# B's attention in pieces of four PSUM banks instead of two

## The chip, the core and the metric

The kernel runs on one core of a Trainium2 chip. The time is the device time of one execution in microseconds (us). A core has five engines that run their own instruction streams and wait for each other through semaphores: TensorE (PE in the profile, its weight loads PEld), VectorE (DVE), ScalarE (ACT), GpSimd (POOL) and SyncE (SP, which here only issues DMA transfers). TensorE writes its results to PSUM, eight banks of 512 fp32 numbers for each of 128 partitions; ACT and DVE read them from there.

## What is computed

Two attention blocks over the same `x` (2048 rows of 1024 numbers), mixed row by row with a gate. Block A is linear attention, block B looks at eight earlier positions at distances 0, 2, ... 14. Both have 32 heads of 32 numbers.

```
g = sigmoid((x * gate_w).sum(-1))
A:  phi(t) = where(t > 0, t + 1, exp(t)) + 1e-6
    kv = einsum("bhsd,bhse->bhde", phi(k), v);  z = phi(k).sum over s
    a  = (phi(q) @ kv) / (phi(q) . z + 1e-6) @ A_wo
B:  idx = pos - (0, 2, ... 14);  logits = q . k[idx] * 32**-0.5, masked where idx < 0
    b  = (softmax(logits) @ v[idx]) @ B_wo
out = g * a + (1 - g) * b
```

## The kernel before

**Products.** Rows are split into even and odd positions (`p` is 0 or 1), so that B's dilated window is eight neighbours within one half. The large matrix products (q, k, v of A and B and the output projections) run in groups with seven block products instead of eight (`Group`: `m1` to `m7`). In the projections, each of the seven is four matmuls of 128x128x512 into a PSUM tile called X or Y; there are two X and two Y tiles of one bank each (pool `ps_pj`). ACT copies X out (`save`, M1s, U2s, U4s), DVE adds Y to such a copy, and the next product of that tile has to wait for it. `run` (line 403) issues a group's products with the last two of the group before it woven in.

**Side work.** Between products, `side` lets small pieces of other work in: B's attention (`attn`), the sums K'V of A (`kv` in `va_group`) and A's outputs (`out` in `qa_out`). Each is a Python generator that issues one piece and then yields two numbers: the delay, in products, before its next piece, and the hold, the number of products for which that piece will keep its PSUM tile. `step` (line 334) takes the first piece that is due and whose tile is free by that count. The counts are only a plan: on the chip, a piece waits by semaphore until the engines have read its PSUM tile. The remaining four banks are two tiles of two banks, `ps_s` and `ps_o`, and a piece takes the one that has been free longest (lines 328 to 332).

**B's attention.** An item is one of eight pairs (chunk pair `nn`, half `p`); it covers eight heads, four in each of two chunks. It handles three stretches `t` of 342 positions. Each is cut into six blocks of 57 (3 `j` x 2 `b`), and a block looks at 64 keys. `scores(t, r)` (line 656) makes the scores of two heads for both chunks: 24 matmuls with 32 rows and 64 columns of the array each, on four array tiles (two heads times two `b`). ACT takes Exp of 684 numbers a partition (line 672), DVE multiplies with the mask (line 674). `pv(t, ch, pts)` (line 677) makes the results of four heads of one chunk: 24 matmuls with V and eight with ones for the denominators, on eight array tiles. ACT takes Ln of the denominators and Exp of minus that (lines 696, 697), DVE multiplies (line 698), SP stores (line 699). Four tiles `PT` are used in turn. So each stretch takes two score pieces and two pv pieces; an item has twelve pieces.

**A's sums and outputs.** `kv` (line 529) adds the sums of 8 column blocks in two pieces, of 12 and 4 matmuls, each followed by a DVE add into `KVacc`. `out` (line 570) does two pieces of four matmuls, each copied by ACT (line 585).

**Order.** The order on TensorE and SP is that of the program text. On ACT, DVE and POOL a scheduler chooses the order at build time; each engine then executes in that order. With every DVE add of the products, `issue_after` keeps deferred sums (`xsums`, `Weights.sums`) behind it. phi (line 501) runs an Exp over 1024 numbers on ACT (line 503) and three operations on DVE for every row tile of A's keys.

The gate's sums `gps` live in a tile of `ps_o` (line 425), and the 20 warm-up matmuls in one of `ps_s` (line 830).

Of the kernel before, what the change touches and what calls it, by code (L numbers as in the profile page):

```python
# [9 lines left out]
ALU = mybir.AluOpType  # L10
# [4 lines left out]
P = 128  # L15
# [13 lines left out]
def kernel(  # L29
# [41 lines left out]
    ps_o = ctx.enter_context(tc.tile_pool(name="ps_o", bufs=1, space=bass.MemoryType.PSUM))  # L71
# [6 lines left out]
    ptp = ctx.enter_context(tc.tile_pool(name="ptp", bufs=1))  # L78
# [147 lines left out]
    PTs = []  # L226
    for i in range(4):
        PTs.append(ptp.tile([P, 2, TW], BF16, name=f"PT{i}"))

# [87 lines left out]
    state = {"credit": 0.0, "prev": None, "steps": 0, "now": 0}  # L317
# [10 lines left out]
    free = {"s": 0, "o": 0}  # L328

    def ps_tile(name):  # L330
        tag = state["tag"]
        return (ps_s if tag == "s" else ps_o).tile([P, 2, 512], F32, name=name, tag=tag)

    def step(force=False):
        seen = set()
        for entry in list(queue):
            if entry[4] in seen:
                continue
            seen.add(entry[4])
            tag = min(free, key=free.get)  # L340
            if not force and (entry[0] > state["now"] or free[tag] > state["now"]):
                continue
            free[tag] = state["now"] + entry[3]
            state["tag"] = tag
            try:
                delay, entry[3] = next(entry[1])
                entry[0] = state["now"] + delay
                state["steps"] += 1
                return True
            except StopIteration:  # L350
                queue.remove(entry)
                return step(force)
        return False
# [67 lines left out]
    def tile_of(pair, i):  # L421
        return (pair // 4) * 8 + (pair % 4) + 4 * i


    gps = ps_o.tile([P, 2, 512], F32, name="gps", tag="o")[:, 0, 0:16]
# [100 lines left out]
    def va_group(w, pair):  # L526
        vs = v_tiles("vA")

        def kv():
            first = kv_state["n"] == 0  # L530
            kv_state["n"] += 1
            last = kv_state["n"] == 8
            yield 0, 3
            for c0, nb in ((0, 2), (6, 1)):
                kps = ps_tile("kps")
                n = 3 if nb == 2 else 2
                for i in range(2):
                    pk = pks[tile_of(pair, i)]
                    for h in range(nb):
                        for k in range(n):  # L540
                            c = c0 + n * h + k
                            nc.tensor.matmul(kps[:, h, k * 132:(k + 1) * 132], lhsT=pk[:, c * P:(c + 1) * P],  # L542
                                             rhs=vs[i][:, 4 * c:4 * c + 4, :].rearrange("p h e -> p (h e)"),
                                             start=i == 0 and k == 0, stop=i == 1, skip_group_check=True)
                src = kps[:, 0:nb, 0:n * 132]
                dst = KVacc[:, c0:c0 + n * nb, :].rearrange("p (a c) e -> p a (c e)", a=nb)
                if first:
                    nc.vector.tensor_copy(out=dst, in_=src)
                else:
                    nc.vector.tensor_tensor(out=dst, in0=src, in1=dst, op=ALU.add)  # L550
                if last and c0:
                    nc.vector.tensor_tensor(out=KVz[:].rearrange("p c (g e) -> p c g e", g=4),
                                            in0=KVacc[:].rearrange("p c (g e) -> p c g e", g=4),
                                            in1=bd[:, None, :, :].broadcast_to([P, 8, 4, 33]), op=ALU.mult)
                yield 2, 3 if kv_state["n"] < 7 else 2

        def done(i):
            if i == 1:
                add_side(2, kv(), 2, "kv", True)
        return Group(row_ops(w, pair), v_final(vs), done)  # L560
# [8 lines left out]
    def qa_out(es, nn, p):  # L569
        def out(i):  # L570
# [7 lines left out]
            for k0 in (0, 2):  # L578
                o = ps_tile("oA")
                for k in range(2):  # L580
                    for j in range(2):
                        nc.tensor.matmul(o[:, k, 132 * j:132 * j + 132],  # L582
                                         lhsT=es[i][:, j, (k0 + k) * P:(k0 + k + 1) * P],
                                         rhs=KVz[:, nn + 4 * j, :], start=True, stop=True)
                oa["copy"] = nc.scalar.copy(out=of[:, k0:k0 + 2].rearrange("p n h e -> p n (h e)"),
                                            in_=o[:, :, 0:264]).ins
                yield 1, 2
# [59 lines left out]
    attn_state = {"pt": 0}  # L647

# [3 lines left out]
    def attn(nn, p, kT, qT, vw):  # L652

        def scores(t, r):
            s = ps_tile("s")
            for ch in range(2):
                for j in range(3):
                    e = (3 * ch + j) * QB  # L660
                    for gi in range(2):
                        g = slice(32 * (2 * r + gi), 32 * (2 * r + gi) + 32)
                        for b in range(2):
                            q0 = q_of(t, j, b)
                            k0 = max(0, q0 - 7)
                            nc.tensor.matmul(s[64 * b:64 * b + 64, gi, e:e + QB],  # L666
                                             lhsT=kT[g, 1024 * ch + k0:1024 * ch + k0 + 64],
                                             rhs=qT[g, 1024 * ch + q0:1024 * ch + q0 + QB],
                                             start=True, stop=True)
            PT = PTs[attn_state["pt"] % 4]  # L670
            attn_state["pt"] += 1
            nc.scalar.activation(out=PT[:], in_=s[:, :, 0:TW], func=ACT.Exp, scale=SCALE)  # L672
            m = maskp[:, 0 if t else 1, :, :].rearrange("p i q -> p (i q)")
            nc.vector.tensor_tensor(out=PT[:], in0=PT[:], in1=m[:, None, :].broadcast_to([P, 2, TW]), op=ALU.mult)  # L674
            return PT

        def pv(t, ch, pts):
            o = ps_tile("o")
            n = 3 * QB
            for j in range(3):  # L680
                for g in range(4):
                    for b in range(2):
                        rows = slice(64 * b, 64 * b + 64)
                        nc.tensor.matmul(o[32 * g:32 * g + 32, b, QB * j:QB * j + QB],  # L684
                                         lhsT=vw[rows, 3 * t + j, 4 * ch + g, :],
                                         rhs=pts[g // 2][rows, g % 2, (3 * ch + j) * QB:(3 * ch + j + 1) * QB],
                                         start=True, stop=True)
            for g in range(4):
                for b in range(2):
                    rows = slice(64 * b, 64 * b + 64)  # L690
                    nc.tensor.matmul(o[32 * g:32 * g + 32, b, n:2 * n], lhsT=ones[rows, :],  # L691
                                     rhs=pts[g // 2][rows, g % 2, ch * n:ch * n + n], start=True, stop=True)
            rB = ofp.tile([P, 3, 2, QB], F32, name="rB", tag="rB", bufs=2)
            oB = ofp.tile([P, 3, 2, QB], BF16, name="oB", tag="oB")
            num, den = (o[:, :, k * n:k * n + n].rearrange("p b (j q) -> p j b q", j=3) for k in range(2))
            nc.scalar.activation(out=rB[:], in_=den, func=ACT.Ln)  # L696
            nc.scalar.activation(out=rB[:], in_=rB[:], func=ACT.Exp, scale=-1.0)  # L697
            nc.vector.tensor_tensor(out=oB[:], in0=num, in1=rB[:], op=ALU.mult)  # L698
            nc.sync.dma_start(out=OB_d[p][2 * nn + ch, :, TW * t:TW * t + TW],
                              in_=oB[:].rearrange("p j b q -> p (j b q)"))  # L700

        last = None
        yield 0, 2
        for t in range(4):
            pts = []
            for r in range(2):
                if t < 3:
                    pts.append(scores(t, r))
                    yield (1, 3) if last else (2, 2)
                if last:  # L710
                    pv(last[0], r, last[1])
                    yield 1, 2 if t + r < 3 else 3
            last = (t, pts)
# [116 lines left out]
    wps0 = ps_s.tile([P, 2, 512], F32, name="wps0", tag="s")  # L830
    for _ in range(20):
        nc.tensor.matmul(wps0[:, 0, 0:256], lhsT=warm[:, 0:P], rhs=warm, start=True, stop=True)
# [143 lines left out]
```

## Time and profile before

| | |
|---|---|
| median of five runs | 479.56 us (479.14 to 481.61) |
| profiled execution: time, span | 479.56 us, 477.8 us |
| instructions profiled | 11675 |
| granted TensorE clock, mean | 0.996 |
| score matmuls (line 666) | 1152 of 32x64 |
| pv matmuls (lines 684, 691) | 1152 and 384 of 64x32 |
| first score, last pv matmul | 67.2 us, 307.8 us |
| A's outputs (line 582) | 315.3 us to 399.8 us |

The span runs from the first to the last recorded instruction; the time contains 1.76 us around it. "Busy" of TensorE adds up the modelled lengths of matmuls that overlap, so it is the start times in the timeline that tell what a piece costs. A line in the list of waits names the waiting instruction, the releaser, and the total, the number and the longest of the waits.

### The profile page before, as it was taken

The page shows a single profiled execution, that of the slowest core. Times are in us where ns is not written, and L with a number is a line of the kernel's source. Part 1 is how long each engine was busy: PE and PEld are TensorE (multiplying, and loading weights), DVE is VectorE, ACT ScalarE, POOL GpSimd, SP SyncE. Part 2 cuts the span into 40 slices and gives each one's busy share as a digit, 9 for nine tenths or more (in the row PEclk, how much of TensorE's full clock was granted, in tenths as well). Part 3 has the DMA queues.
Part 4 walks back from the last instruction along what each step waited for, and adds up shares of the span by engine and source line. Part 5 has one row for each costly group of instructions (what it writes and reads, how often), then busy time and mean ns, then how long its engine had stood idle before and what let it go on. Part 6 is the DMA issues. An engine that isn't in the chain of part 4 may idle for free.

```text
span 477.8 us, 11675 instructions
## 1 busy us (share of the span) xinstructions
PE 455.4 (95%) x4855; PEld 214.1 (45%) x4916; DVE 282.3 (59%) x504; ACT 242.0 (51%) x423; POOL 64.3 (13%) x145
## 2 busy tenths in 40 slices
PE   7989999998999999999999999999998799999997
PEld 4445444443444444444444444544443344444443
DVE  0546766589556585565755646686975765154411
ACT  1333347657577484774846848455554334221321
POOL 8000000000000000000000000018874315000000
PEclk9999999999999999999999999999999899999999
DMA  7899712680303303034030343662239761599211
GB/s 177 191 222 253 245 24 69 207 173 25 73 9 88 91 24 73 3 85 101 17 81 1 83 103 112 186 192 66 67 83 211 148 143 56 100 170 204 79 42 47
DMA packets 118037, 51.64 MB, mean 108 GB/s; under 512 B 78048, under 2 KB 115936, under 8 KB 117984
## 3 DMA queue, kind: packets, MB, share of 16 engines
q1 hardware_dynamic: 117888, 50.88, 45.5%
q8 instruction: 38, 0.62, 0.6%
q0 software_dynamic: 96, 0.01, 0.2%
q14 instruction: 15, 0.12, 0.1%
HBM read 25.69 MB, written 16.79 MB: 89 GB/s over the span
## 4 chain that ended last, share of the span: by engine, by line
PE 55%; DVE 8%; POOL 4%; issue 2%; DMA 2%; ACT 2%; SPq 1%; POOLq 0%; DVEq 0%; ACTq 0%
PE X L255 27%; PE Y L255 21%; POOL obA L595 3%; PE s L666 2%; PE o L684 1%; PE Q L626 1%; PE kps L542 1%; DMA oT<-OA_d 1%; DVE eq L636 1%; DMA WS<-in_A_wqkv_dram 1%; DVE oS L783 1%; PE oA L582 1%; DVE oB L698 1%; SPq L775 1%; DVE eA L509 1%
## 5 line engine op out<-in xcount | busy, mean ns | idle before, releaser
L255 PEld LDWEIGHTS <-xT 128*128 128x128 bf16 (+1 forms) x352 | 31.6, 98 | 34.7 <-issue 0.3
L255 PE MATMUL X<-T,SS 128*128 128x512 f16 x176 | 45.4, 380 | 0.0
L626 PE MATMUL Q<-xT,WS 128*128 128x512 bf16 x184 | 44.6, 379 | 0.5 <-DMA OB_d<-oB 0.2
L264 ACT COPY U4s<-X 128x512 f32<-128x512 f32 x40 | 23.2, 581 | 37.9 <-PE X L255 37.9
L672 ACT ACTIVATE PT<-s 128x684 bf16<-128x684 f32 x48 | 35.4, 738 | 11.9 <-PE s L666 11.8
L255 PEld LDWEIGHTS <-WS 128*128 128x128 bf16 (+1 forms) x288 | 26.5, 98 | 29.7 <-issue 0.5
L255 PE MATMUL Y<-W,xT 128*128 128x512 bf16 (+1 forms) x152 | 39.1, 380 | 0.0
L255 PE MATMUL Y<-xT,WS 128*128 128x512 bf16 (+1 forms) x144 | 37.1, 380 | 0.0
L255 PE MATMUL X<-SS,TS 128*128 128x512 f16 x144 | 37.0, 379 | 0.0
L698 DVE TENSOR_TENSOR oB<-o,rB 128x342 bf16<-128x342 f32 x48 | 24.5, 510 | 19.9 <-ACT rB L697 19.3
L674 DVE TENSOR_TENSOR PT<-PT,maskp 128x684 bf16<-128x684 bf16 x48 | 24.6, 512 | 19.5 <-ACT PT L672 19.0
L255 PEld LDWEIGHTS <-SS 128*128 128x128 f16 x264 | 23.2, 98 | 25.7
L255 PEld LDWEIGHTS <-oT 128*128 128x128 bf16 (+1 forms) x192 | 18.7, 98 | 24.5 <-DMA oT<-OA_d 2.1
L696 ACT ACTIVATE rB<-o 128x342 f32<-128x342 f32 x48 | 22.2, 462 | 14.4 <-PE o L691 14.1
L255 PEld LDWEIGHTS <-TS 128*128 128x128 f16 x216 | 19.7, 98 | 21.1
L264 ACT COPY M1s<-X 128x512 f32<-128x512 f32 x40 | 23.2, 579 | 9.9 <-PE X L255 9.9
L264 ACT COPY U2s<-X 128x512 f32<-128x512 f32 x40 | 23.3, 582 | 7.7 <-PE X L255 7.6
L626 PEld LDWEIGHTS <-WS 128*128 128x128 bf16 x192 | 17.7, 98 | 17.0
L697 ACT ACTIVATE rB<-rB 128x342 f32<-128x342 f32 x48 | 23.5, 489 | 1.5
L255 PE MATMUL X<-T,oS 128*128 128x512 f16 x96 | 23.9, 394 | 0.0
L631 ACT ACTIVATE eq<-Q 128x512 bf16<-128x512 f32 x24 | 14.3, 597 | 17.7 <-PE Q L626 16.7
L255 PE MATMUL Y<-T,xT 128*128 128x512 f16 x88 | 22.7, 380 | 0.0
(132 smaller groups left out, 769.6 us busy)
## 6 DMA issues: line engine op xcount, KB each, us to landing
OB_d<-oB SPq DMA_DIRECT2D x48, 85.5 KB, 2.0
V_d<-va SPq DMA_DIRECT2D x16, 256.0 KB, 2.7
WS<-in_B_wqkv_dram SPq DMA_DIRECT2D x16, 256.0 KB, 4.1
W<-in_A_wqkv_dram SPq DMA_DIRECT2D x8, 512.0 KB, 6.0
OA_d<-obA SPq DMA_DIRECT2D x16, 256.0 KB, 2.3
out_dram<-osb SPq DMA_DIRECT2D x32, 128.0 KB, 1.8
oT<-OB_d SPq DMA_DIRECT2D x12, 256.0 KB, 4.8
vw<-V_d SPq DMA_DIRECT2D x8, 288.0 KB, 4.3
```

Source lines behind the costliest of these rows:

```text
L255: nc.tensor.matmul(ps[:], lhsT=lhsT, rhs=rhs, start=start and kc == 0, stop=kc == self.nk - 1, skip_group_check=True)
L264: nc.scalar.copy(out=s[:], in_=ps[:])
L509: nc.vector.tensor_tensor(out=e, in0=e, in1=t, op=ALU.add)
L595: nc.gpsimd.tensor_tensor(out=ob[:, k:k + 2], in0=of[:, k:k + 2, :, 0:32], in1=rec[:, k:k + 2].broadcast_to([P, 2, 8, 32]), op=ALU.mult)
L626: nc.tensor.matmul(ps[:], lhsT=w.W[:, kc, j * P:j * P + P], rhs=xT[p][:, kc, i, :], start=kc == 0, stop=kc == 7, skip_group_check=True)
L631: nc.scalar.activation(out=es[i][:, j, :], in_=ps[:], func=ACT.Exp)
L666: nc.tensor.matmul(s[64 * b:64 * b + 64, gi, e:e + QB], lhsT=kT[g, 1024 * ch + k0:1024 * ch + k0 + 64], rhs=qT[g, 1024 * ch + q0:1024 * ch ...
L672: nc.scalar.activation(out=PT[:], in_=s[:, :, 0:TW], func=ACT.Exp, scale=SCALE)
L674: nc.vector.tensor_tensor(out=PT[:], in0=PT[:], in1=m[:, None, :].broadcast_to([P, 2, TW]), op=ALU.mult)
L696: nc.scalar.activation(out=rB[:], in_=den, func=ACT.Ln)
L697: nc.scalar.activation(out=rB[:], in_=rB[:], func=ACT.Exp, scale=-1.0)
L698: nc.vector.tensor_tensor(out=oB[:], in0=num, in1=rB[:], op=ALU.mult)
```

## The change

All side work shares one PSUM tile of four banks (`side_ps`); `ps_o` is gone, and `free` becomes one number. `scores(t)` makes the scores of all four heads of both chunks at once: 48 matmuls on eight array tiles (four heads times two `b`), one Exp and one mask multiply over 1368 numbers a partition. `pv(t, PT)` makes both chunks: 48 and 16 matmuls, one Ln and one Exp over 684 numbers, two multiplies over 342, one store. An item has six pieces with a planned hold of three products (the first score two). `PT` becomes two tiles of double size from a rotating pool, `rB` one buffer instead of two, `oB` two of double size instead of three. `kv` and `out` make one piece of what were two. The gate and the warm-up share the first big tile, in different banks.

```diff
+    def side_ps(name):
+        return ps_s.tile([P, 4, 512], F32, name=name, tag="s")
...
-            tag = min(free, key=free.get)
-            if not force and (entry[0] > state["now"] or free[tag] > state["now"]):
+            if not force and (entry[0] > state["now"] or state["free"] > state["now"]):
                 continue
-            free[tag] = state["now"] + entry[3]
-            state["tag"] = tag
+            state["free"] = state["now"] + entry[3]
...
-            for c0, nb in ((0, 2), (6, 1)):
-                kps = ps_tile("kps")
...
+            kps = side_ps("kps")
+            for i in range(2):
+                pk = pks[tile_of(pair, i)]
+                for c in range(8):
+                    nc.tensor.matmul(kps[:, c // 2, c % 2 * 132:c % 2 * 132 + 132], lhsT=pk[:, c * P:(c + 1) * P],
...
+            yield 2, 2
...
+            o = side_ps("oA")
+            for k in range(4):
+                for j in range(2):
+                    nc.tensor.matmul(o[:, k, 132 * j:132 * j + 132], lhsT=es[i][:, j, k * P:(k + 1) * P],
+                                     rhs=KVz[:, nn + 4 * j, :], start=True, stop=True)
+            oa["copy"] = nc.scalar.copy(out=of[:].rearrange("p n h e -> p n (h e)"), in_=o[:, :, 0:264]).ins
+            yield 1, 2
...
+        def scores(t):
+            s = side_ps("s")
             for ch in range(2):
                 for j in range(3):
                     e = (3 * ch + j) * QB
...
+                    for b in range(2):
+                        q0 = q_of(t, j, b)
+                        k0 = max(0, q0 - 7)
+                        for g in range(4):
+                            nc.tensor.matmul(s[64 * b:64 * b + 64, g, e:e + QB],
+                                             lhsT=kT[32 * g:32 * g + 32, 1024 * ch + k0:1024 * ch + k0 + 64],
+                                             rhs=qT[32 * g:32 * g + 32, 1024 * ch + q0:1024 * ch + q0 + QB],
                                              start=True, stop=True)
+            PT = ptp.tile([P, 4, TW], BF16, name="PT", tag="PT")
             nc.scalar.activation(out=PT[:], in_=s[:, :, 0:TW], func=ACT.Exp, scale=SCALE)
...
+        def pv(t, PT):
+            o = side_ps("o")
             n = 3 * QB
+            for ch in range(2):
+                for j in range(3):
+                    for g in range(4):
+                        for b in range(2):
...
+                            nc.tensor.matmul(o[32 * g:32 * g + 32, 2 * ch + b, QB * j:QB * j + QB],
...
+            rB = ofp.tile([P, 4, n], F32, name="rB", tag="rB", bufs=1)
+            oB = ofp.tile([P, 2, 3, 2, QB], BF16, name="oB", tag="oB", bufs=2)
+            nc.scalar.activation(out=rB[:], in_=o[:, :, n:2 * n], func=ACT.Ln)
             nc.scalar.activation(out=rB[:], in_=rB[:], func=ACT.Exp, scale=-1.0)
...
+            for ch in range(2):
...
+                nc.vector.tensor_tensor(out=oB[:, ch], in0=num, in1=r, op=ALU.mult)
...
         for t in range(4):
...
+            if t < 3:
+                PT = scores(t)
+                yield (1, 3) if last else (3, 3)
+            if last:
+                pv(*last)
+                yield 1, 3
+            last = (t, PT)
```

## The prediction

> **What bounds the kernel now.** I read the page's busy shares first, then the waits of TensorE, then the timeline of one attention item (140 to 165 us) and the groups by line.
>
> ```profile
> PE 455.4 (95%) x4855; PEld 214.1 (45%) x4916; DVE 282.3 (59%) x504; ACT 242.0 (51%) x423; POOL 64.3 (13%) x145
> ```
>
> TensorE is busy for 95% of the span; no other engine passes 59%. The waits of TensorE (waiter, releaser, total us, times, longest) are small, so a change pays only in TensorE's own time, or in what it makes TensorE wait:
>
> ```profile
> PE oA L582 <- DVE eq L509: 3.1, 2, 2.5
> ...
> PE oA L582 <- DVE eq L636: 1.9, 6, 0.4
> ...
> PE o L684 <- DVE oB L698: 1.6, 3, 1.1
> ```
>
> In the timeline (start, length, engine, group) the price of one attention piece can be read off:
>
> ```profile
> 142.78 0.81 PE L255 MATMUL X<-W,xT 128*128 128x512 bf16 x3 [0.16 <-issue]
> ...
> 143.53 0.38 PE L666 MATMUL s<-qT,kT 32*64 32x57 bf16 x24
> ...
> 143.84 1.04 PE L255 MATMUL Y<-W,xT 128*128 128x512 bf16 x4
> ...
> 144.71 1.03 PE L255 MATMUL X<-SS,WS 128*128 128x512 f16 x4
> ...
> 145.67 0.28 PE L684 MATMUL o<-PT,vw 64*32 64x57 bf16 x24
> ...
> 145.76 0.26 PE L691 MATMUL o<-PT,ones 64*32 64x171 bf16 x8
> ...
> 145.95 1.04 PE L255 MATMUL X<-T,SS 128*128 128x512 f16 x4
> ```
>
> A product of four matmuls takes 0.863 us (143.84 to 144.71, 0.216 a matmul). The X product that starts its second matmul at 142.78 is streamed at 142.78 + 3 x 0.216 = 143.43, and the next product starts at 143.84: a score piece costs **0.41**. Likewise 144.71 + 0.863 = 145.57 to 145.95: a pv piece costs **0.38**. Only 0.19 of the first (0.38 less one matmul's 0.19) and some 0.12 of the second are the stream of small matmuls; the rest is the way into the small tiles and back.
>
> The groups by line give the engines that empty the pieces (busy us, mean ns):
>
> ```profile
> L672 ACT ACTIVATE PT<-s 128x684 bf16<-128x684 f32 x48 | 35.4, 738 | 11.9 <-PE s L666 11.8
> L697 ACT ACTIVATE rB<-rB 128x342 f32<-128x342 f32 x48 | 23.5, 489 | 1.5
> L696 ACT ACTIVATE rB<-o 128x342 f32<-128x342 f32 x48 | 22.2, 462 | 14.4 <-PE o L691 14.1
> L503 ACT ACTIVATE eA<-tA 128x1024 bf16<-128x1024 bf16 x16 | 16.8, 1052 | 1.2 <-DVE tA L237 1.0
> ...
> L698 DVE TENSOR_TENSOR oB<-o,rB 128x342 bf16<-128x342 f32 x48 | 24.5, 510 | 19.9 <-ACT rB L697 19.3
> ...
> L237 DVE TENSOR_TENSOR tA<-Y,U2s 128x512 bf16<-128x512 f32 x8 | 5.5, 682 | 0.0
> ```
>
> **Part 1, TensorE's own time.** The matmuls are the same in number; 48 score and 48 pv pieces become 24 and 24. Before, 24 score matmuls run on 4 array tiles, six deep, in 0.19. Afterwards 48 run on 8 tiles, again six deep. The pv piece already runs on 8 tiles (24 matmuls, three deep, in 0.09), so I take the score piece at 0.41. The new pv piece adds three waves of 57 columns (0.09) and a second wave of 171 columns (three times as long as 57, so 0.09): 0.38 + 0.18 = 0.56. Before: 48 x 0.41 + 48 x 0.38 = 37.9. After: 24 x 0.41 + 24 x 0.56 = 23.3. **Gain 14.6.** The KV sums (128 matmuls) and A's outputs (128) keep number and tile size; merging them saves TensorE nothing.
>
> **Part 2, the new wait.** There were two PSUM tiles of two banks in turn; now one of four. The piece behind a pv piece needs ACT's Ln, ACT's Exp and both DVE multiplies of that pv piece done. From L696 and L672 ACT's slope is (738 - 462) / 342 = 0.81 ns an element, so Ln on 684 elements takes 0.46 + 0.28 = 0.74 and Exp 0.49 + 0.28 = 0.77. The two multiplies are two of L698, overlapping by 0.08: 0.94. The changed program puts three products, 2.59 us, between pieces.
>
> With nothing in ACT's way: Ln begins 0.67 after the first pv matmul (0.50 in the trace at 149.06 to 149.56, and 0.18 of longer piece), then 0.74 + 0.03 + 0.77 + 0.04 + 0.94 + 0.06 = 3.25 after it. TensorE is back 0.46 + 2.59 + 0.09 = 3.14 after it. Wait 0.1, for 8 pieces (the second pv of an item to the third): 0.8.
>
> The first pv of an item is worse. In the changed program's order it stands right behind the last product of a key-projection group of A (Y), and ACT's queue holds the second phi Exp (L503) ahead of the Ln. From the end of Y's stream: 0.20 until DVE may start, its add 0.68, 0.03, phi Exp 1.05 less 0.09 overlap, Ln 0.74, 0.03, Exp 0.77, 0.04, then DVE's last phi add delays the multiplies by 0.17, 0.94, 0.06: 4.6. TensorE arrives after 0.56 + 2.59 + 0.09 = 3.24. **Wait 1.4**, in 7 items (the first item has no phi beside it): 9.8. In two of them a weight sum of 0.42 stands ahead of DVE's add, in another a sum of 1.2: 2.0 more. The last KV sum stands three products behind the last pv piece while phi work begins: 0.1 to 1.4, I take 1.3. Together 0.8 + 9.8 + 2.0 + 1.3 = **13.9**. Removed: the 1.6 of the view of waits, and 0.2 before a KV sum. **Loss 12.1.** Behind the waiting score piece stands all of TensorE's queue.
>
> Score pieces themselves are covered: their Exp takes 0.74 + 0.57 = 1.31, the room is 2.59. An X copy behind it waits 1.31 + 0.58 at the most against 1.73 of two products: 0.2 now and then, not counted; without that cover it is 24 x 0.2 = 5.
>
> **Part 3, the rest at nothing.** A's output copies become one of 1.04 (528 elements 0.60, plus 528 x 0.83 ns) within two products' 1.73; only where a drain puts two pieces side by side TensorE waits about 1.3, and half of the 1.9 of L636 waits goes. Net 0, bounds -1.5 and +1.5. The gate matmuls and the warm-up share the big tile; the gate is read long before the first score at 67 us. SP issues 24 output DMAs where it issued 48, each waiting for its oB, with the weight and V loads behind them. An item now spans 15 products from its first score to its last pv piece, before some 17, so nothing on that queue comes later, and its loads lead their use by whole groups. POOL's order is the same; its memsets of kT wait for the last scores, which come earlier. The larger mask multiply (0.51 + 684 x 0.52 ns = 0.87) leads its pv by six products.
>
> **Sum.** -14.6 + 12.1 = -2.5 on the profiled run, which took 479.56 with a span of 477.8 and is also the median of the five runs shown. I add 0.2, because four more tiles have to be started in each of the 24 score pieces (the pv piece starts a tile each 2 to 4 ns): **477.3**. Its own range from the bounds above: 475 to 480.
>
> **The cost that no row shows.** A score piece was 48 instructions in one burst (24 weight loads, 24 matmuls), a pv piece 64; they become 96 and 128. The pv row shows 64 instructions in 0.12 us, and full-size work resumes on time behind it, so 64 come at once. Whether 128 do, nothing shows. The tightest stretch is two pv pieces with one product between (136 instructions from 119.12 to 120.50): 10.1 ns an instruction if none lay ready, 19 ns if 64 did. Lower bound: nothing. Upper: 24 x ((32 x 19 - 190) + (64 x 19 - 300)) ns = 32 us. I take nothing, because the nearest row, the 64-burst, shows no slowing towards its end.
>
> [...]
>
> **Rivals.** (a) The burst outruns the queue, the slower side. Place: the last 32 instructions of each score piece, the last 64 of each pv piece. At 10.1 ns: 24 x (0.13 + 0.35) = 11.5, so 489. It decides from about 6 ns on, where the gain is gone. For: no burst over 64 exists. Against: no sign inside 64. Chance 0.25. (b) The longer ACT pieces also delay X copies, the 5 us named above: 482. For: ACT's order holds 1.05 + 0.74 + 0.77 in a row. Against: ACT is 51% busy, and before its copies M1s, U2s and U4s it idles 9.9, 7.7 and 37.9 us. Chance 0.08. (c) The first pv's wait is half as long, since DVE's or ACT's hand-overs overlap more: 477.3 - 6 = 471. For: two of the three waits of L684 were 0.25. Against: each link of the chain needs the one before. Chance 0.12. (d) The likeliest, 0.55.
>
> **The numbers.** No change means within 0.5%, about what a measurement of this kernel can tell: 477.2 to 482. The likeliest lies on that border: 0.24 faster, 0.31 same; (c) adds 0.12 faster; (a) 0.22 slower and 0.03 same; (b) 0.08 slower. Faster 0.36, same 0.34, slower 0.30. The range goes from 474 to 489, leaving out half of (a) and most of (c).
>
> **What would show it.** Right: score groups of 48 with about 0.2 between first and last start, pv groups followed by full work 0.2 later, and a wait of TensorE's L647 on DVE's oB of 11 to 13 us over 7 or 8 times. Wrong: starts within a group that spread out behind the 64th instruction (a); idle TensorE before X behind ACT (b); L647 waiting under 6 us (c).

## The result, and the profile after

The changed kernel takes 483.87 us (median of 42 runs, 479.95 to 487.38), the kernel before 480.75 (79 runs, 476.90 to 483.72): a ratio of 1.006, 95% interval 1.0045 to 1.0074. It is slower by 3 us, where 477.3 was forecast.

The profiled execution took 485.55 us with a span of 483.6, 6 us above that of before. Of these, 2.7 us arise ahead of the first score piece (69.91 us against 67.19), in a part that the change does not touch. From the first score to the last matmul's start it is 409.9 us against 406.7: 3.2 us, as in the medians. This is the part to explain. 2.5 of the 3.2 arise before the first plain query group (line 610, line 626 before), where B's attention runs, and 0.75 behind it, up to the last matmul of A's outputs.

The page after, its line of engines and the groups that empty the pieces (busy us, mean ns, idle time before):

```profile
PE 452.0 (93%) x4840; PEld 220.5 (46%) x4916; DVE 277.0 (57%) x472; ACT 234.3 (48%) x335; POOL 63.5 (13%) x145
...
L652 ACT ACTIVATE PT<-s 128x1368 bf16<-128x1368 f32 x24 | 31.5, 1311 | 27.1 <-PE s L647 27.1
...
L654 DVE TENSOR_TENSOR PT<-PT,maskp 128x1368 bf16<-128x1368 bf16 x24 | 20.8, 867 | 20.8 <-ACT PT L652 20.8
...
L682 DVE TENSOR_TENSOR oB<-o,rB 128x342 bf16<-128x342 f32 x48 | 22.3, 507 | 7.1 <-ACT rB L678 7.1
```

ACT and DVE did what the sums expected of them: Exp 1.311 us (forecast 1.31), mask 0.867 (0.87). Against the 0.738 and 0.512 us of before for 684 numbers that is 0.84 and 0.52 ns for each of the 684 more. ACT was busy for 7.7 us less. TensorE's own list of waits after:

```profile
PE s L647 <- DVE oB L682: 9.3, 7, 2.0
PE oA L568 <- DVE eq L500: 3.1, 1, 3.1
PE Y L250 <- DVE tq L232: 2.2, 1, 2.2
...
PE oA L568 <- ACT of L570: 1.2, 1, 1.2
PE kps L529 <- DVE oB L682: 1.2, 1, 1.2
```

The forecast wait is there, on the line that was named, seven times. The timeline around one of them (PE, ACT and DVE rows, others left out) shows its chain:

```profile
141.99 0.54 PE L665 MATMUL o<-PT,vw 64*32 64x57 bf16 x48
142.10 0.69 DVE L232 TENSOR_TENSOR tA<-Y,U2s 128x512 bf16<-128x512 f32 x1 [0.45 <-PE Y L250]
...
142.65 1.04 PE L250 MATMUL Y<-xT,WS 128*128 128x512 f16 x4
...
142.82 1.06 ACT L494 ACTIVATE eA<-tA 128x1024 bf16<-128x1024 bf16 x1
...
143.79 0.73 ACT L677 ACTIVATE rB<-o 128x684 f32<-128x684 f32 x1
...
144.55 0.78 ACT L678 ACTIVATE rB<-rB 128x684 f32<-128x684 f32 x1
...
145.50 0.93 DVE L682 TENSOR_TENSOR oB<-o,rB 128x342 bf16<-128x342 f32 x2
...
146.48 0.57 PE L647 MATMUL s<-qT,kT 32*64 32x57 bf16 x48 [1.06 <-DVE oB L682]
```

DVE's add ends at 142.79, phi's Exp takes ACT until 143.88, and Ln, Exp and the multiplies follow end to end until 146.43. The score piece starts at 146.48, 1.06 us late.

The price of the pieces is in the same rows: the pv piece starts at 141.99, and the full-size product behind it only at 142.65. Taken over all pieces from the recorded starts (median time between the full-size matmuls around a piece, less one matmul's 0.216):

```
                score piece    pv piece    both, per stretch
before            0.405          0.380     2 x 0.405 + 2 x 0.380 = 1.570
after             0.594          0.760         0.594 + 0.760     = 1.354
forecast          0.41           0.56
```

Hence 24 x 0.216 = 5.2 us gained, not 14.4. The starts within a piece show where it went (ns from the piece's first matmul; every fourth matmul of a typical one, and the next full-size matmul):

```
before, pv     0  14  39  53  69  82  98 112 | next product 288
after, score   0  14  54  66  86  99 119 130 | 237 270 304 337 | next product 500
after, pv      0  14  39  53  69  82  98 112 | 225 258 291 325 358 391 440 474 | next product 667
```

Up to the 32nd matmul (with its weight load 64 instructions) the new pv piece runs exactly as the old one, and the score piece close to that, 2 ns an instruction. Then comes a pause of some 0.1 us, and from there on 4 matmuls, eight instructions, take 33 ns in the main: 4.2 ns an instruction.

So the balance is 5.2 us gained, 10.5 us (9.3 + 1.2) of new waits and 1.8 of removed ones: +3.5, against +3.2 in this part of the trace and +3.1 in the medians. It leaves out A's stage, where the waits for ACT and DVE grew by 1.5 us and one for a transfer (oT) fell by 0.6; with these it is +4.4, so the balance closes to about 1 us.

### The profile page after: what moved, and what is told of

Its sections match the earlier page's. It is cut to its first block, busy times and chain, and to the rows that moved or that the text cites. A ratio compares the mean times of both kernels' runs of the same rounds, so it can differ in the third digit from the quotient of the medians.

```text
span 483.6 us, 11454 instructions
## 1 busy us (share of the span) xinstructions
PE 452.0 (93%) x4840; PEld 220.5 (46%) x4916; DVE 277.0 (57%) x472; ACT 234.3 (48%) x335; POOL 63.5 (13%) x145
## 4 chain that ended last, share of the span: by engine, by line
PE 77%; DVE 9%; POOL 4%; issue 3%; DMA 3%; SPq 2%; ACT 2%; POOLq 0%; DVEq 0%; another core or an unknown queue 0%; ACTq 0%
PE X L250 36%; PE Y L250 27%; PE Q L610 4%; PE K L471 3%; POOL obA L579 3%; PE s L647 2%; PE kps L529 2%; PE o L665 2%; DVE oB L682 1%; DVE eA L500 1%; DMA W<-in_B_wqkv_dram 1%; DVE eA L499 1%; POOL rec L573 1%; DVE tA L498 1%; PE oA L568 1%
## 5 line engine op out<-in xcount | busy, mean ns | idle before, releaser
L250 PEld LDWEIGHTS <-xT 128*128 128x128 bf16 (+1 forms) x352 | 33.2, 98 | 38.8 <-issue 0.5
L652 ACT ACTIVATE PT<-s 128x1368 bf16<-128x1368 f32 x24 | 31.5, 1311 | 27.1 <-PE s L647 27.1
L610 PE MATMUL Q<-xT,WS 128*128 128x512 bf16 x185 | 42.9, 379 | 0.3
L250 PE MATMUL Y<-W,xT 128*128 128x512 bf16 (+1 forms) x138 | 37.8, 385 | 1.5 <-issue 1.1
L250 PEld LDWEIGHTS <-SS 128*128 128x128 f16 x264 | 24.9, 99 | 29.1 <-issue 1.7
L654 DVE TENSOR_TENSOR PT<-PT,maskp 128x1368 bf16<-128x1368 bf16 x24 | 20.8, 867 | 20.8 <-ACT PT L652 20.8
L259 ACT COPY U2s<-X 128x512 f32<-128x512 f32 x40 | 23.3, 583 | 10.2 <-PE X L250 10.1
L682 DVE TENSOR_TENSOR oB<-o,rB 128x342 bf16<-128x342 f32 x48 | 22.3, 507 | 7.1 <-ACT rB L678 7.1
L250 PE MATMUL X<-W,SS 128*128 128x512 bf16 x80 | 23.1, 393 | 0.4
L250 PE MATMUL Y<-W,oT 128*128 128x512 bf16 (+1 forms) x96 | 22.7, 379 | 0.0
```

What stands on the lines that cost most here:

```text
L250: nc.tensor.matmul(ps[:], lhsT=lhsT, rhs=rhs, start=start and kc == 0, stop=kc == self.nk - 1, skip_group_check=True)
L259: nc.scalar.copy(out=s[:], in_=ps[:])
L610: nc.tensor.matmul(ps[:], lhsT=w.W[:, kc, j * P:j * P + P], rhs=xT[p][:, kc, i, :], start=kc == 0, stop=kc == 7, skip_group_check=True)
L682: nc.vector.tensor_tensor(out=oB[:, ch], in0=num, in1=r, op=ALU.mult)
```

## The experiments

Two causes were to be tested: the wait (10.5 us) and the long burst (9.2 us missing). Ratios are to the kernel before, run beside each experiment on the same chip.

**Room behind the first pv piece: five products.** The plan of the next piece is two products later, nothing else:

```diff
-                yield (1, 3) if last else (3, 3)
+                yield (1, 5 if last[0] == 0 else 3) if last else (3, 3)
```

> The changed kernel, with five products instead of three behind the first pv piece of each item. Theory (the changed kernel's loss is the wait of the next score piece for that pv piece's DVE multiplies, 9.3 us in 7 waits, and nothing else moves): TensorE's wait of the score line on oB falls from 9.3 to at most 1 us and the time by 7 to 9 us, to 475 to 477, below the kernel before. Rival (the wait only stands where TensorE would have lost the time anyway, because ACT and DVE are behind there): the wait moves to another line and the time stays within 2 us of 483.9.

Measured: 474.05 us, ratio 0.986 (0.981 to 0.992), a little below the expected range. Neither the score line nor the KV sum waits for oB any more. The windows from 65 to 300 us show it (start:end us, length, then busy us of PE, PEld, DVE, ACT and POOL with instructions, granted clock, DMA share, GB/s); first the kernel before:

```profile
65.00:300.00 235.00, 229.26 (x3536) 106.36 (x3571) 151.51 (x279) 155.08 (x280) 4.77 (x29) 1.00 0.30 74
```

the changed kernel:

```profile
65.00:300.00 235.00, 221.54 (x3476) 110.05 (x3527) 147.12 (x248) 148.15 (x209) 4.97 (x29) 1.00 0.30 74
```

and the changed kernel with five products:

```profile
65.00:300.00 235.00, 234.62 (x3582) 114.49 (x3581) 149.51 (x253) 148.54 (x215) 4.96 (x29) 1.00 0.32 79
```

TensorE, idle for 13.5 of these 235 us in the changed kernel, is idle for 0.4. Of the 13.5, 9.3 are the waits of the score line, and 2.1 stand in the list of waits as `issue`, where the trace lacks a matmul behind a piece. From the first score to the last matmul's start it takes 399.4 us instead of 409.9: 10.5 less, as much as the waits of the score line and the KV sum. The wait was on the path, and the room was free to give: an item's pieces still end well before the next item's (the second item's last piece starts at 123.3 us, the third's first at 134.5).

**Four products.** The same line with 4 in place of 5.

> The changed kernel with four products instead of three behind the first pv piece of each item. Theory (the wait is a chain of fixed length against the products that run beside it, 0.863 us each): the waits of 1.06, 1.48 and 1.99 us become 0.2, 0.6 and 1.1, together 4 x 0.2 + 2 x 0.6 + 1.1 = 3.1 instead of 9.3, and the time 6 us less, 477 to 478.5. Rival (the wait goes away with five products because the next item's pieces fall beside other work): with four it stays near 9 or is gone altogether.

Measured: 478.02 us, ratio 0.996 (0.992 to 0.999), with these waits:

```profile
PE s L647 <- DVE oB L682: 3.3, 7, 1.1
...
PE kps L529 <- DVE oB L682: 2.1, 1, 2.1
```

Waits and time are as expected: each product of room takes its own length (0.86 us) off each wait of the score line, 9.3 to 3.3 to 0, as a chain of fixed length against a planned number of products would. The KV sum's wait did not shrink with four products; it went from 1.2 to 2.1 us.

**phi behind the pv piece.** The plan stays at three products; on ACT, the second phi of a key group is put behind Ln and Exp, and its operations on DVE come later with it:

```diff
-            phi(e[:], ts[i][:])
+            later(2, lambda: phi_behind(e[:], ts[i][:])) if i else phi(e[:], ts[i][:])
...
+        with tc.issue_after(ln[0]) if ln[0] else nullcontext():
+            nc.scalar.activation(out=e, in_=t, func=ACT.Exp)
...
+            ln[0] = nc.scalar.activation(out=rB[:], in_=rB[:], func=ACT.Exp, scale=-1.0).ins
```

> The changed kernel, with the second phi of each key-projection group of A put behind the Ln and the Exp of the first pv piece on ACT (and its DVE operations behind the two multiplies). Theory (phi's Exp of 1.05 us ahead of the Ln is the link that makes the wait): the seven waits of 1.06 to 1.99 us lose about 1.05 + 0.17 each; 9.3 falls to about 1.5 us and the time to about 476. Rival (the wait is that of the chain Ln, Exp, multiplies in itself, or of DVE's sums ahead): the wait stays above 6 us and the time above 481. If X copies behind the moved phi come late, TensorE shows a new wait on ACT of some 0.3 us in each of seven items.

Measured: 474.55 us, ratio 0.988 (0.983 to 0.994). The same place in its timeline, ACT, DVE and PE rows:

```profile
141.61 0.74 ACT L686 ACTIVATE rB<-o 128x684 f32<-128x684 f32 x1
142.38 0.77 ACT L687 ACTIVATE rB<-rB 128x684 f32<-128x684 f32 x1
143.06 1.04 ACT L506 ACTIVATE eA<-tA 128x1024 bf16<-128x1024 bf16 x1
143.19 0.93 DVE L691 TENSOR_TENSOR oB<-o,rB 128x342 bf16<-128x342 f32 x2 [0.16 <-ACT rB L687]
...
144.20 0.57 PE L656 MATMUL s<-qT,kT 32*64 32x57 bf16 x48
```

The multiplies no longer stand behind phi and end at 144.12. In TensorE's list of waits the score line's falls from 9.3 us to

```profile
PE s L656 <- DVE oB L691: 1.1, 3, 0.7
```

while no new wait of X on ACT appears and the KV sum's 1.2 us stay. phi was the link: its Exp of 1.06 us on ACT, with the operations on DVE that moved along. That two different cures, more room and a shorter chain, give the same time is what the theory of the chain asks for.

**Longer bursts in the kernel before.** Its pieces keep two banks; six score matmuls and four pv matmuls of each piece are done twice:

```diff
+            for ch, j, gi, b in [(0, 0, gi, b) for gi in range(2) for b in range(2)] + [(0, 1, 0, b) for b in range(2)]:
...
+            for g in range(2):
+                for b in range(2):
+                    rows = slice(64 * b, 64 * b + 64)
+                    nc.tensor.matmul(o[32 * g:32 * g + 32, b, 0:QB], lhsT=vw[rows, 3 * t, 4 * ch + g, :],
```

> The kernel before, with work added inside its pieces: 6 score matmuls of each score piece done twice (30 matmuls with their weight loads, 60 instructions) and 4 pv matmuls of each pv piece done twice (36, that is 72 instructions). Theory (TensorE takes 64 instructions of a burst at 2 ns each, then pauses for about 0.1 us and goes on at 4.2 ns an instruction): the score piece grows from 0.405 by 0.02 to 0.05 us and shows no pause; the pv piece grows from 0.38 by 0.10 to 0.15 us, with a pause of about 0.1 us behind its 32nd matmul; together 48 x 0.16 = 6 to 9 us more than before. Rival (the changed pieces cost more because of the array tiles or banks they use, not because of their length): the pv piece grows by 0.02 to 0.03 us like the score piece, no pause, together 2 to 3 us.

Measured: 485.99 us, ratio 1.010 (1.007 to 1.013), 5.7 us more. Starts as above:

```
score, 30      0  53  86 118 151 183 215 247 | next product 370
pv, 36         0  13  39  52  68  81  97 111 | 225 | next product 377
```

The pv piece shows the pause behind its 32nd matmul, at the same 225 ns, in two banks: four more small matmuls cost 0.090 us (0.470 against 0.380), a little below its range. The score piece grows by 0.058, a little above its range; it runs at 8.2 ns a matmul from the fifth matmul on, on its four array tiles, before the change as well, so no pause can be seen there. Together 48 x 0.148 = 7.1 us; from the first score to the last pv matmul the trace has 6.3 more. The repeated pv matmuls stand behind the wide ones on the same array tiles, which alone might hold them up; but in the changed kernel the 33rd matmul has only narrow ones before it and comes at the same 225 ns.

**Other orders.** Two tests of whether the break belongs to particular matmuls. In the first the score loops are turned:

```diff
-            for ch in range(2):
-                for j in range(3):
-                    e = (3 * ch + j) * QB
-                    for b in range(2):
...
+            for j in range(3):
+                for b in range(2):
+                    q0 = q_of(t, j, b)
+                    k0 = max(0, q0 - 7)
+                    for ch in range(2):
+                        e = (3 * ch + j) * QB
```

> The changed kernel, with the 48 matmuls of a score piece in another order (query stretch, key half, chunk, head instead of chunk, query stretch, key half, head), so that the second chunk's matmuls are spread over the piece. Theory (the break is in the count of instructions): starts still break between the 32nd and the 33rd matmul by about 0.1 us and go on at 8.3 ns a pair; piece cost 0.59 us, time 483 to 485. Rival (the break belongs to what the 33rd matmul touches: the third stretch of the second chunk, a place in a bank, a weight that is not loaded yet): the break moves to another matmul or is gone, and the piece cost falls by 0.1 us or more.

In the second the loop of the 16 matmuls with ones stands ahead of that with V, otherwise unchanged:

> The changed kernel, with the 16 matmuls of the denominators (171 columns each) ahead of the 48 numerators of a pv piece instead of behind them. Theory (behind the 64th instruction the burst goes at the rate at which instructions arrive, 4.2 ns each, whatever they compute): the last start of a piece stays at about 0.49 to 0.50 us behind the first, and the piece ends 0.03 to 0.05 us earlier only because its last matmul is a short one: 0.71 to 0.73 us instead of 0.76, 24 x 0.04 = 1 us in all; the waits of the score line stay at about 9, since phi's Exp still stands ahead of the Ln. Time 482 to 484. Rival (the array's streaming sets the length of the pv piece): the wide matmuls, started at once, cover the arrival of the others and the piece falls to 0.56 us or less, the time by 4 to 5 us, to 479.

Measured: 482.97 us (one run) and 484.03 (ratio 1.008, 1.005 to 1.011).

```
score, turned    0  27  53  80  88 112 120 144 | 236 269 311 354 | next product 500
pv, ones first   0  13  84  97 162 175 188 204 | 270 304 346 380 413 446 480 513 | next product 667
```

In the turned score piece the break stays behind the 32nd matmul. With the wide matmuls first, the first 32 spread out over 0.20 us and the pause shrinks into that; the next product comes at 667 ns in both orders. Theory and rival of the second order both missed: the piece did not fall to 0.56 us, and it did not end earlier by even the 0.04 us of its shorter last matmul. The length did not follow what the matmuls compute, 667 ns in either order; that it is set by when the instructions arrive, the next product's included, was not shown. The starts of the next product are then one rule: 377 ns for 72 instructions, 500 for 96, 667 for 128, that is 5.2 ns for each instruction of the piece in all three. At 64 it would be 333; the old pv piece took 288.

**Both.** Five products, and the ones first:

> The changed kernel with five products behind the first pv piece of an item, and with the denominators' matmuls first. Theory: the two gains add, since one takes away a wait and the other TensorE's own time: 474.0 less 1.0, about 473, and no wait of the score line on oB. Rival (the shorter piece is given back as a wait, or the room that was added is lost elsewhere): the time of the kernel with five products alone, 474 to 475.

Measured: 475.57 us, ratio 0.991 (0.988 to 0.994), no better than five products alone (0.986, 0.981 to 0.992). The gains did not add, and the rival's time was the nearer one, but because the order gained nothing that could be given back: the piece is at 0.76 as before.

**The pv merge undone on TensorE.** In the four-bank tile, the chunks' 32 matmuls stand in two bursts, one product apart; Ln, Exp and multiplies come once, behind the second:

```diff
-            for ch in range(2):
+            def chunk(ch):
...
+            chunk(0)
+            state["half"] = rest
+            later(1, half)
...
-                yield (1, 3) if last else (3, 3)
+                yield (1, 5 if last[0] == 0 else 4) if last else (3, 3)
```

> The changed kernel with the merge of the pv pieces undone on TensorE alone: the two chunks of a pv piece (32 matmuls, 64 instructions each) stand in two bursts with one product between, in the same four banks; ACT and DVE still empty both at once, behind the second. Five products behind the first burst of an item's first pv piece, four behind the second's. Theory (a burst of up to 64 instructions is free of the pause, so the merge of pv pieces saved nothing): no start later than 0.13 us behind the first of its burst, each burst costs 0.38, together 0.76 as in the one piece of 64 matmuls; the score line's wait falls to between 1 and 4 us by the one product of room more. Time 475 to 479. Rival (the four-bank tile or the use of all banks slows the pv matmuls themselves): the bursts cost more than 0.45 each, and the time stays above 481.

Measured: 492.77 us, ratio 1.026 (1.022 to 1.031). The burst is as the theory had it: last of the listed starts at 0.110 us, 0.380 each, 0.760 together, on eight array tiles and in the four-bank tile. So merging pv pieces gave TensorE nothing. The time missed by 14 us and stands on the rival's side of its bound, but not for the rival's reason: the bursts' price is the old one. With the longer plan the last pieces move out of the stage that has room. The last pv matmul stands at 323.1 us, 21.6 behind the start of the plain query groups (line 617), against 13.3 with five products alone, and the waits are now there, on lines of that stage:

```profile
PE Q L617 <- DVE eq L627: 6.0, 4, 1.5
PE kps L536 <- DVE oB L698: 3.7, 6, 1.1
PE oA L575 <- ACT of L577: 3.3, 2, 2.1
PE oA L575 <- ACT ofv L577: 2.4, 2, 1.2
```

The granted clock was lower there as well: 0.87 from 340 to 380 us, where the kernel with five products had 0.96, worth up to 40 x 0.09 = 3.6 us by estimate; whether the waits brought it about was not tested. With six products behind the first burst, in place of five, the same split deadlocks.

**The score merge undone on TensorE.** In the kernel with five products, head pairs in two bursts of 24, one product apart, one Exp and one mask behind the second:

```diff
+            def pair(r):
...
+                        for g in (2 * r, 2 * r + 1):
...
+            pair(0)
+            state["half"] = rest
+            later(1, half)
```

> The kernel with five products behind the first pv piece, and with the merge of the score pieces undone on TensorE alone: head pairs 0 and 1 (24 matmuls each on four array tiles, as before the change) stand in two bursts with one product between, in the same four banks; one Exp and one mask multiply behind the second. Theory (the merged score piece is the only gain of the change on TensorE, 2 x 0.405 - 0.594 = 0.216 us a time): the bursts cost 0.40 each and the time is 24 x 0.216 = 5.2 us above the kernel with five products alone: 479 to 480, as the kernel before. Rival (the score merge gains little on the chip too, and five products gain by something else): the time stays within 2 us of 474 to 475.

and the same with one more product ahead of an item's first pv piece, `(3, 4)` in place of the last `(3, 3)`:

> The kernel with five products behind the first pv piece and with the score pieces in two bursts, with one more product between an item's second score piece and its first pv piece. Theory (in the run without it, 6.0 us went where that pv piece waits for the scores' Exp, which stood one product later and behind a phi Exp; the bursts themselves cost 0.404 each): the wait of the pv line on PT, 6.0 us in 7 times, falls to under 1 us, the time from 490.5 to 482 to 485; what is left above 479 is X copies late behind ACT, 3 us. Rival (the split score piece costs TensorE more than its two bursts): the wait falls and the time stays above 488.

Measured: 490.52 us (ratio 1.020, 1.016 to 1.024) and 493.20 (1.029, 1.023 to 1.034). Both times missed, and for the first its rival (within 2 us of 474 to 475) did too. The bursts cost 0.404 and 0.405 each, as before the change: 24 x (2 x 0.404 - 0.594) = 5.1 us. Most of the rest of the 16 us in the first is waits, since the scores' Exp now stands one product later:

```profile
PE o L679 <- ACT PT L663: 6.0, 7, 0.9
...
PE X L250 <- ACT U4s L259: 2.9, 7, 0.4
```

From the first score to the first plain query group it takes 242.2 us against 227.1, 15.1 more; 5.1 + 6.0 + 2.9 = 14.0 of it are named. One more product removes the 6.0, as the theory said, and then the items run late as in the pv split:

```profile
PE Q L617 <- DVE eq L627: 6.0, 4, 1.5
PE oA L575 <- ACT of L577: 3.3, 2, 2.1
PE oA L575 <- ACT ofv L577: 2.4, 2, 1.2
```

The time (482 to 485 was expected) is on the rival's side of its bound, but not for the rival's reason: the bursts' price is unchanged. The last pv matmul stands 20.9 us behind the start of line 617, and the clock from 340 to 380 us was 0.91. So the 5.1 us rest on the pieces' measured price, not on the time of a whole kernel: neither merge could be undone alone without moving the plan.

## Why the prediction was wrong, step by step

**The step that failed** is "The cost that no row shows": "I take nothing, because the nearest row, the 64-burst, shows no slowing towards its end." It cost 14.4 - 5.2 = 9.2 us, enough to turn a gain of 2.3 into a loss. A row that ends at 64 instructions cannot show what the 65th does. Its bounds, nothing to 32 us, held; the choice between them was wrong. Rival (a) had the place: the last 32 instructions of a score piece and the last 64 of a pv piece. Its cause, a burst that outruns a queue, no run shows; the runs show a pause of some 0.1 us and then 4.2 ns an instruction in place of 2. Its price, 11.5, was near the 9.2: its 0.13 us for a score piece and 0.35 for a pv piece were 0.18 and 0.20 on the chip, since an instruction behind the break takes 4.2 ns, not 10.1, and a pause comes on top. The nearness is partly luck: at 4.2 ns the rival's own formula gives no cost at all (32 x 4.2 = 134 against 190, 64 x 4.2 = 269 against 300), and it has no pause.

**Part 1.** The score piece was forecast at 0.41 and took 0.594, the pv piece at 0.56 and 0.760: 24 x (0.18 + 0.20) = 9.2. The array's side of the estimate, waves on eight tiles, was not what failed: the first 32 matmuls of each piece keep to the pace of the old pv piece (the 29th at 130 and 112 ns, in the old one at 112).

**Part 2** had the right place, chain and count, and was oversized: 12.1 net against 10.5 - 1.8 = 8.7. The seven first pv pieces were given 9.8 + 2.0 and took 9.3; the second pv piece's 0.1 in eight items did not appear; the KV sum was given 1.3 and took 1.2. Four of the seven waits are 1.06, not 1.4: the pv piece itself is 0.2 longer than forecast, and this runs beside the chain.

**Part 3.** The net 0 is within its bounds: from the first plain query group to the last matmul of A's outputs it takes 98.5 us against 97.75, 0.75 more with the KV sum's wait among them, though A's stage waits 3.1 + 2.2 + 1.2 us where 5.0 were before, 1.5 more. The covered score pieces cost no X copy (rival b): no such row is in the waits. Rival (c), half the wait, was wrong: the first pv pieces took 9.3 of the 11.8 they were given.

**The sum.** With the piece prices as measured, 477.3 + 9.2 would have been 486.5, and with Part 2 as measured 3.4 less: 483.1, against 483.87. The sum starts from the 479.56 of the profiled run; from the 480.75 of all 79 runs it would be 484.3.

## What to carry to other kernels

Merging short pieces between large products saved TensorE only 0.216 us a stretch (1.354 against 1.570) here, where a merged piece passed 64 instructions, loads counted: beyond that the next product started 5.2 ns after the piece's first matmul for each of its instructions, so that 48 + 48 instructions became cheaper as 96 (0.594 against 0.81 us) and 64 + 64 as 128 did not (0.76 either way). Merging also halved the buffers in turn: look for what stands ahead, on the engine that empties the piece, of the work that empties it, and give the next piece as many products of room as that chain is long. Here two more products at one piece of each item turned +0.6% into -1.4%, while the two kernels with one more at further pieces had their last items in a stage that had no room for them, and waits of 6.0 us on its line 617.

## What the runs showed of the hardware

In pieces on eight array tiles, TensorE started the first 32 loads and matmuls of 57 columns, 64 instructions, at about 2 ns each (the 32nd matmul 0.12 to 0.14 us after the first in the profile of after); the 33rd came 0.22 to 0.24 us after the first, and the later ones every 8.3 ns in the main, 4.2 ns an instruction. The break stayed there in another order of the score matmuls, in score and pv pieces, and in two banks as in four. On four array tiles, in the score pieces of before, matmuls came every 8.2 ns from the fifth on, and no burst there was longer than 60 instructions. Every matmul here has its own weight load, so the runs cannot tell 64 instructions from 32 matmuls. What happens in the pause was not settled.

The stage ahead of the first score ran at a granted clock of 1.00 in the profile of before and of 0.95 in that of after (10 to 65 us), and was 2.7 us longer. It is not the change: in the profile of the split pv pieces, with the same code there as after, the clock was 1.00 and the first score stood at 67.80 us; with five products it was 0.96 and 70.06. A difference of single profiles below 3 us should therefore be taken from the first score on, and the clock watched there too: from 360 to 400 us it was 0.96 both before and after, but 1.00 in the profile with turned scores, which has the same waits of the score line and the same price of the pieces as after and took 407.0 us from the first score on, not 409.9.
